# Batch 0 of an attention and mixer kernel written out in program order, with its loads in another order

## The chip, the cores and the metric

The kernel runs on one core of a Trainium2 chip. The metric is device time in microseconds (us), one launch. A core has a matmul engine (PE, with its weight loads shown as PEld), three engines for elementwise work (DVE, ACT, POOL) and SP, which only issues DMAs here. Each engine works through its own instructions in order and waits for others by semaphores. SP and POOL issue DMAs into two different queues; both queues are served by the same 16 DMA engines. Only POOL's DMAs change the type (here from float32 to bfloat16).

## What is computed

Eight batches of causal attention with a decay bias (8 heads, 576 positions, 64 dims), and a mixer on the result:

```python
scores = scale * q @ k.T
cum = cumsum(maximum(s, 0), axis=-1)
bias = minimum(-(cum[:, :, :, None] - cum[:, :, None, :]), 0)
attn = softmax(where(causal, -1e9, scores + bias))
x = (attn @ v)                    # heads side by side: (8, 576, 512)
u = x + (x.T @ U @ V).T           # U (576, 32), V (32, 576): along the sequence
out = u + maximum(u @ w_ch1, 0) @ w_ch2     # w_ch1 (512, 2048), w_ch2 (2048, 512)
```

## The kernel before

**Stages.** Work goes by pairs of heads, four pairs to a batch, 32 in all.

- `scores(n)` (L245): for each head of pair n, matmuls of q and k from a slot into PSUM, with exp on ACT (L264, L273, L277, L279) and the causal mask as a minimum with `keep` on DVE (L265, L285). Results lie in one of two tiles `pT`. The decay bias is in the matmul: rows 64 to 67 of a slot hold the cumulated decay of q and k in split precision, so the contraction is over 68 rows. Nine matmuls, 1600 columns a head.
- `values(n)` (L296): 15 matmuls of 65 columns a head with v, where a column of ones gives the sum; DVE divides (L315, L316) into `x_sb`.
- `seqmix(b)` (L325), once a batch: U (L329), a copy `ux` on DVE (L337), then for each of four blocks a transposition and V (L342, L350) and a DVE cast into `uT` (L358; L378 for the last 64 positions).
- `chanmix(g)` (L386), for 512 tokens: 16 blocks of w1 (four matmuls of 512 columns each, L391) with ReLU on ACT (L398), then four times 16 matmuls with w2 (L404), the residual (L415), a copy on DVE and the store. It is a generator, and its steps are used as filling: `run` (L437) takes one step of filling after each step of scores, values or seqmix; `fill_with(n)` takes n steps at once.

**q and k.** Batch 0's q and k are loaded with positions on 72 partitions (`load_first`, L76) and transposed on PE (`first_transposes`, L202), with copies into the slots on ACT for heads 0 to 3 and on DVE for heads 4 to 7. From batch 1 on, `load_qk` (L85) loads four heads (a group) as 8 DMAs; `place` (L224) transposes 32x32 blocks on DVE (four instructions a group, L234) into `turned` and moves them into a slot by 8 DMAs on SP (L240), with the decay rows from HBM (L226). There are three slots of four heads, four buffers for groups and two for `turned`.

**The beginning.** s is loaded (SP, L67); DVE clamps, scans and splits it (L140 to L147), ACT makes the negated row (L143); SP moves the rows of batch 0's eight heads into slots 0 and 1 (L150), one DMA a head, and the others to HBM (L155). On POOL's queue stand: q and k of heads 0 and 1, 2 and 3, 4 to 7; v of batch 0 (`load_v`, L167: five DMAs of 128-byte rows, after a memset of the tile); U and V; w1 whole (2 MB, L190); q and k of batch 1; w2 whole (2 MB, L192); v of batch 1. POOL's DMAs take turns on eight semaphores, and one is issued only when that which had its semaphore before has landed. `spin` (L129) issues matmuls on constants whose result nobody reads.

**What sets the order.** Each engine's order is set by the framework's scheduler, which takes the source order as a start and moves instructions by its own estimates. So in the built program the first scores stand ahead of the last transposes of heads 4 to 7, the memsets of `v_slot` (L163, L164) stand between the steps of the decay rows on DVE, and group 2's transposes (L234) stand behind `ux`.

Of the kernel before, what the change touches and what calls it, by code (L numbers as in the profile page):

```python
# [20 lines left out]
def kernel(  # L21
# [40 lines left out]

# [4 lines left out]
    nc.sync.dma_start(out=s_sb, in_=s.rearrange("b h s -> (b h) s"))  # L67

# [5 lines left out]
    )  # L74

# [9 lines left out]
    def load_qk(b):  # L85
        for g in range(2 * b, 2 * b + 2):
            qk_t[g] = loads.tile([128, 2, ST * D], BF16, tag="qk_sd", name="qk_sd", bufs=4)
# [6 lines left out]

    load_first(0, 2)
    identity = consts.tile([128, 128], BF16)
    make_identity(nc, identity)
    load_first(2, 2)
    load_first(4, 4)

    keep = consts.tile([128, 4, 128], BF16)
    nc.gpsimd.memset(keep, 3.0e38)
    nc.gpsimd.affine_select(
        out=keep,
        in_=keep,
        compare_op=ALU.is_ge,
        fill=0.0,
        base=0,
        pattern=[[0, 4], [1, 128]],
        channel_multiplier=-1,  # L110
    )


    PW = 1664
    pTs = [consts.tile([128, 2, PW], BF16, name=f"pT{i}") for i in range(2)]
    nc.vector.memset(pTs[1][:, 0, 0:640], 1.0)
    nc.vector.memset(rows[:, 0:3, 0, :], 1.0)
    nc.vector.memset(rows[:, 3, 1, :], 1.0)
    for pT in pTs:
        nc.vector.memset(pT[:, :, 1600:], 1.0)  # L120
    NSLOT = 3

    SK = 5 * 128
    slots = [consts.tile([128, 4, S + SK], BF16, name=f"slot{i}") for i in range(NSLOT)]
    for slot in slots:
        nc.vector.memset(slot[:KA, :, 2 * S :], 0.0)


    def spin(n):  # L129
        for _ in range(n):  # L130
            nc.tensor.matmul(
                pscore(),
                lhsT=pTs[1][:, 0, 512:640],
                rhs=pTs[1][:, 0, 0:512],
                start=True,
                stop=True,
            )


    nc.vector.tensor_scalar(s_sb, s_sb, 0.0, 1.0 / scale, op0=ALU.max, op1=ALU.mult)  # L140
    nc.vector.tensor_tensor_scan(cum, s_sb, s_sb, 0.0, op0=ALU.add, op1=ALU.max)
    rest = s_sb
    nc.scalar.mul(rows[:, 3, 0, :], cum, -1.0)  # L143
    nc.vector.tensor_copy(rows[:, 0, 1, :], cum)
    nc.vector.tensor_sub(rest, cum, rows[:, 0, 1, :])
    nc.vector.tensor_copy(rows[:, 1, 1, :], rest)
    nc.vector.tensor_sub(rows[:, 2, 1, :], rest, rows[:, 1, 1, :])  # L147
    for n in range(PB):
        for hh in range(2):
            nc.sync.dma_start(  # L150
                out=slots[n // 2][D:KA, 2 * (n % 2) + hh, 0 : 2 * S],
                in_=rows[2 * n + hh : 2 * n + hh + 1].rearrange("n r c s -> n r (c s)"),
            )
    rows_hbm = nc.dram_tensor("rows_hbm", (4, BH, 2, S), BF16, kind="Internal").ap()
    nc.sync.dma_start(  # L155
        out=rows_hbm[:, ds(2 * PB, BH - 2 * PB)].rearrange("r n c s -> n r c s"),
        in_=rows[2 * PB :],
    )

    v_slots = []  # L160
    for i in range(3):
        vt = consts.tile([128, 5, H, D + 1], BF16, name=f"v_slot{i}")
        nc.vector.memset(vt[:, :, :, D : D + 1], 1.0)  # L163
        nc.vector.memset(vt[64:, 4, :, :], 0.0)  # L164
        v_slots.append(vt)

    def load_v(b):  # L167
        vt = v_slots[b % 3]
        for t in range(4):
# [5 lines left out]
            out=vt[:64, 4, :, 0:D], in_=v[b, :, 512:576, :].rearrange("h p d -> p h d")  # L175
        )

    load_v(0)
    U_sb = consts.tile([128, 5, 128], BF16)
    nc.vector.memset(U_sb, 0.0)  # L180
    V_sb = consts.tile([128, S], BF16)
# [269 lines left out]
    for n in range(PB):  # L451
        for _ in first_transposes(n):
            spin(1)
# [56 lines left out]
```

## Time and profile before

| | us |
|---|---|
| median of 4 runs | 409.2 (408.21 to 412.18) |
| profiled execution | 409.13 |
| its span, first to last instruction | 407.4 |
| PE busy | 374.2 (92%) |
| DVE, ACT, POOL busy | 195.8, 194.7, 106.6 |
| first scores of batch 0 start on PE | 19.27 |
| first matmul of seqmix(0) | 40.84 |
| first matmul of chanmix(0) | 45.98 |
| first scores of batch 1 start on PE | 56.63 |

The span is counted from the first instruction; the profiled execution's time has 1.7 us around it. A matmul's end is modelled, so PE's busy time is rather too long for short matmuls. In lists of waits a line reads: who waited, for whom, us in total, how often, the longest. In a timeline a line reads: start, us, engine, line, operation, tile written and read, shape, count, and in brackets the idle time before it with what ended it. The granted clock of PE is a share of its full clock.

### The profile page before, as it was taken

What the parts mean: (1) busy time and instruction counts of PE and PEld (TensorE: products, weight loads), DVE (VectorE), ACT (ScalarE), POOL (GpSimd) and SP (SyncE); (2) the same over time, 40 slices, a digit from 0 to 9 for tenths busy, and PEclk for the clock granted to TensorE, in tenths of its full rate; (3) what the DMA queues carried; (4) which work ended last, traced back from release to release, by engine and by line L of the source; (5) the groups of instructions that cost most, each with busy time, mean ns of one, the idle gap of its engine ahead of it and who ended that gap; (6) DMA issues with size and microseconds to landing.
All of it is one profiled execution on the core that took longest, in us unless ns stands there. A gap on an engine that the chain in (4) does not pass through costs nothing.

```text
span 407.4 us, 7986 instructions
## 1 busy us (share of the span) xinstructions
PE 374.2 (92%) x3121; PEld 212.7 (52%) x3176; DVE 195.8 (48%) x394; ACT 194.7 (48%) x378; POOL 106.6 (26%) x171
## 2 busy tenths in 40 slices
PE   6188849999989999999999999999999999999996
PEld 2067425565545555556555655555555554444442
DVE  8168821789588654754574734432444331002011
ACT  4096237653855087327732683358336630630610
POOL 8527328785763764300040000000000000000000
PEclk9557978999999999999999999999999999999999
DMA  8999999999997997572156311220011002001002
GB/s 109 153 224 113 181 159 168 117 209 197 182 157 128 178 174 101 80 101 76 34 62 104 89 35 29 71 69 2 0 53 53 2 0 79 26 26 64 16 27 77
DMA packets 80524, 37.91 MB, mean 93 GB/s; under 512 B 64422, under 2 KB 74822, under 8 KB 80486
## 3 DMA queue, kind: packets, MB, share of 16 engines
q0 software_dynamic: 65680, 18.44, 50.8%
q1 hardware_dynamic: 14806, 18.96, 16.7%
q8 instruction: 25, 0.41, 0.4%
q14 instruction: 13, 0.11, 0.1%
HBM read 37.51 MB, written 9.95 MB: 116 GB/s over the span
## 4 chain that ended last, share of the span: by engine, by line
PE 62%; DMA 21%; DVE 7%; POOL 5%; issue 2%; ACT 1%; SPq 1%; DVEq 0%; POOLq 0%; ACTq 0%
PE pwork L404 25%; PE pwork L391 21%; DMA v_slot<-in_v_dram 9%; PE pscore L253 6%; DVE turned L234 5%; DMA w_sb<-in_moe_w_ch_dram 4%; PE pwork L306 4%; DMA slot<-turned 4%; POOL qk_sd L90 2%; DMA qk_sd<-in_k_dram 2%; DMA hT<-in_k_dram 2%; PE pwork L329 2%; PE pwork L415 2%; PE pwork L342 1%; POOL v_slot L170 1%
## 5 line engine op out<-in xcount | busy, mean ns | idle before, releaser
L391 PE MATMUL pwork<-uT,w_sb 128*128 128x512 bf16 x548 | 141.2, 383 | 3.3 <-DVE x_sb L316 1.9
L404 PE MATMUL pwork<-w_sb,hT 128*128 128x512 bf16 x553 | 138.5, 379 | 1.2
L398 ACT ACTIVATE hT<-pwork 128x512 bf16<-128x512 f32 x144 | 88.0, 612 | 79.7 <-PE pwork L391 76.8
L253 PE MATMUL pscore<-slot 68*128 68x128 bf16 (+4 forms) x576 | 70.9, 254 | 15.3 <-DMA slot<-hT 9.9
L264 ACT ACTIVATE pT<-pscore 128x512 bf16<-128x512 f32 x64 | 38.6, 603 | 96.5 <-PE pscore L253 96.4
L404 PEld LDWEIGHTS <-hT 128*128 128x128 bf16 x576 | 52.3, 98 | 48.1
L391 PEld LDWEIGHTS <-w_sb 128*128 128x128 bf16 x576 | 51.3, 98 | 48.1 <-DVE x_sb L316 2.4
L253 PEld LDWEIGHTS <-slot 68*128 68x128 bf16 x576 | 45.5, 103 | 45.6 <-issue 17.9
L424 DVE COPY o_sb<-pwork 128x512 f32<-128x512 f32 x36 | 24.7, 687 | 79.8 <-PE pwork L415 79.8
L234 DVE STREAM_TRANSPOSE turned<-qk_sd 128x576 bf16<-128x576 bf16 x56 | 59.5, 1121 | 4.9 <-DMA slot<-turned 2.7
L265 DVE TENSOR_TENSOR pT<-pT,keep 128x512 bf16<-128x512 bf16 x64 | 26.7, 421 | 65.4 <-ACT pT L264 65.2
L306 PEld LDWEIGHTS <-pT 128*128 128x128 bf16 x960 | 40.0, 100 | 14.5 <-issue 0.7
L273 ACT ACTIVATE pT<-pscore 128x512 bf16<-128x512 f32 x64 | 39.0, 610 | 13.0 <-PE pscore L253 11.0
L306 PE MATMUL pwork<-v_slot,pT 128*128 128x65 bf16 x960 | 43.1, 197 | 0.3
L170 POOL DMA_DIRECT2D v_slot<-in_v_dram x32 | 28.3, 897 | 55.5 <-PE pwork L306 52.9
L90 POOL DMA_DIRECT2D qk_sd<-in_k_dram x56 | 31.5, 568 | 31.4 <-DMA v_slot<-in_v_dram 18.4
L277 ACT ACTIVATE pT<-pscore 128x512 bf16<-128x512 f32 x64 | 39.3, 614 | 0.1
L90 POOL DMA_DIRECT2D qk_sd<-in_q_dram x56 | 31.7, 581 | 17.2 <-DMA w_sb<-in_moe_w_ch_dram 9.7
L316 DVE TENSOR_TENSOR x_sb<-pwork,rec 128x320 bf16<-128x320 f32 x64 | 30.9, 488 | 1.9
L358 DVE CAST uT<-pwork 128x512 bf16<-128x512 f32 x32 | 21.3, 684 | 9.8 <-PE pwork L350 9.2
L315 DVE RECIPROCAL rec<-pwork 128x5 f32<-128x5 f32 x64 | 11.5, 183 | 29.2 <-PE pwork L306 28.9
L415 PEld LDWEIGHTS <-uT 128*128 128x128 bf16 x144 | 11.1, 98 | 8.5
(54 smaller groups left out, 155.1 us busy)
## 6 DMA issues: line engine op xcount, KB each, us to landing
out_dram<-o_sb SPq DMA_DIRECT2D x36, 256.0 KB
slot<-turned SPq DMA_DIRECT2D x112, 72.0 KB
v_slot<-in_v_dram POOLq DMA_DIRECT2D x32, 128.0 KB, 6.9
w_sb<-in_moe_w_ch_dram POOLq DMA_DIRECT2D x2, 2048.0 KB, 16.4
qk_sd<-in_q_dram POOLq DMA_DIRECT2D x56, 72.0 KB, 4.6
qk_sd<-in_k_dram POOLq DMA_DIRECT2D x56, 72.0 KB, 4.3
v_slot<-in_v_dram POOLq DMA_DIRECT2D x8, 64.0 KB, 7.5
rows_hbm<-hT SPq DMA_DIRECT2D x1, 504.0 KB
```

The costliest lines, as they stand in the source:

```text
L90: nc.gpsimd.dma_start(out=qk_t[g][ds(32 * a, 32), c, :].rearrange("p (n f) -> p n f", n=6), in_=src[b, 4 * (g % 2) + a].rearrange("(n p t) ...
L170: nc.gpsimd.dma_start(out=vt[:, t, :, 0:D], in_=v[b, :, ds(t * 128, 128), :].rearrange("h p d -> p h d"),)
L234: nc.vector.transpose(turned[:, c, e].rearrange("p (n m t) -> p n t m", n=6, t=3), src[:, c].rearrange("p (n t e d) -> p e n t d", n=6, t= ...
L253: nc.tensor.matmul(dst, lhsT=kT[:, ds(j * 128, 128)], rhs=qT[:, lo:hi], start=True, stop=True,)
L264: nc.scalar.activation(pT[:, hh, 0:512], diag, EXP, scale=scale)
L273: nc.scalar.activation(pT[:, hh, 512:1024], far, EXP, scale=scale)
L277: nc.scalar.activation(pT[:, hh, 1024:1536], mid, EXP, scale=scale)
L306: nc.tensor.matmul(po[:, i, :], lhsT=pT[:, hh, ds(spot(j, i), 128)], rhs=vt[:, j, h, :], start=(j == 0), stop=(j == i), skip_group_check=True,
L316: nc.vector.tensor_tensor(x_sb[:, :, ds(h * D, D)], po[:, :, 0:D], rec.to_broadcast([128, 5, D]), op=ALU.mult,)
L391: nc.tensor.matmul(f1, lhsT=w1_sb[:, kt, ds(nf * 128, 128)], rhs=uT[:, kt, ds(g * 512, 512)], start=(kt == 0), stop=(kt == 3),)
L398: nc.scalar.activation(hT[:, nf, :], f1, RELU)
L404: nc.tensor.matmul(f2, lhsT=hT[:, nf, ds(i * 128, 128)], rhs=w2_sb[:, nf, :], start=(nf == 0), stop=False, skip_group_check=True,)
```

## The change

- Everything from the first load to the end of batch 0's seqmix stands in a block in which the scheduler keeps the program's order on every engine. What follows is scheduled as before, and may be moved in between.
- Memsets of ones write pairs as one FP32 value. The spins read a tile of their own, `warm`, and write one PSUM tile, `idle`, which is held to the end of batch 0, so that three of the four `pwork` buffers are left for it. There are 48 spins (10, then 2 + 2 + 8, then one after each step that is run `warmly`) where there were 16.
- The q k loads stand ahead of the identity on POOL. Transposes and copies of heads 0 to 3 stand ahead of the first scores, those of heads 4 to 7 after the scores of pairs 0 and 1. One copy in two of heads 2 and 3 is on DVE.
- The decay rows' DMAs stand ahead of the memsets of `v_slot`, and so ahead of the loads of v.
- w1 and w2 are four tiles of 512 KB each, loaded by four DMAs each (w1 in 1 KB rows, where it had 4 KB). The order of loads is: v of batch 0, U, V, two blocks of w1, q and k of batch 1, two blocks of w1, v of batch 1, w2.
- `turned` holds q and k of one half of the dims side by side, so that a row of its DMA is 2304 bytes, not 1152. Groups have three buffers, not four.
- Eight steps of chanmix(0), not four, are run before batch 1.

In the built program, DVE's order in batch 0 after pair 0's masks is: copies of heads 4 and 5, masks of pair 1, copies of heads 6 and 7, rec and x_sb of pair 0, two masks of pair 2, two transposes of group 2 (they wait for q), the last mask of pair 2, rec and x_sb of pair 1, masks of pair 3 with the other two transposes of group 2 (they wait for k) between them, rec and x_sb of pairs 2 and 3 with two transposes of group 3 between, ux, a transpose of group 3, the uT casts, the last transpose of group 3.

```diff
+    warm = consts.tile([128, 512], BF16)
...
+    w1_sb = [consts.tile([128, 4, 512], BF16, name=f"w1_sb{i}") for i in range(4)]
+    w2_sb = [consts.tile([128, 4, DM], BF16, name=f"w2_sb{i}") for i in range(4)]
...
+    ones_pair = float.fromhex("0x1.007f00p+0")
+
+    def ones(ap):
+        nc.vector.memset(ap.bitcast(FP32), ones_pair)
...
-            qk_t[g] = loads.tile([128, 2, ST * D], BF16, tag="qk_sd", name="qk_sd", bufs=4)
+            qk_t[g] = loads.tile([128, 2, ST * D], BF16, tag="qk_sd", name="qk_sd", bufs=3)
...
+    def load_w1(i):
+        nc.gpsimd.dma_start(
+            out=w1_sb[i],
+            in_=moe_w_ch1[:, ds(i * 512, 512)].rearrange("(kt kp) n -> kp kt n", kp=128),
+        )
...
-        for c in range(2):
-            for e in range(2):
+        for e in range(2):
+            for c in range(2):
                 nc.vector.transpose(
-                    turned[:, c, e].rearrange("p (n m t) -> p n t m", n=6, t=3),
+                    turned[:, e, c].rearrange("p (n m t) -> p n t m", n=6, t=3),
                     src[:, c].rearrange("p (n t e d) -> p e n t d", n=6, t=3, e=2)[:, e],
                 )
-        for a in range(4):
-            for e in range(2):
+            for a in range(4):
                 nc.sync.dma_start(
-                    out=slot[ds(32 * e, 32), a, 0 : 2 * S].rearrange("p (c s) -> p c s", c=2),
-                    in_=turned[ds(32 * a, 32), :, e, :],
+                    out=slot[ds(32 * e, 32), a, 0 : 2 * S],
+                    in_=turned[ds(32 * a, 32), e].rearrange("p c s -> p (c s)"),
                 )
...
-                    lhsT=w1_sb[:, kt, ds(nf * 128, 128)],
+                    lhsT=w1_sb[nf // 4][:, kt, ds(nf % 4 * 128, 128)],
...
-                    rhs=w2_sb[:, nf, :],
+                    rhs=w2_sb[nf // 4][:, nf % 4, :],
...
-    spin(8)
-    for n in range(PB):
-        for _ in first_transposes(n):
-            spin(1)
-    for n in range(PB):
-        drain(scores(n))
-        if n > 0:
-            drain(values(n - 1))
+    copy_a, copy_v = nc.scalar.copy, nc.vector.tensor_copy
+    with tc.manual_schedule():
+        nc.sync.dma_start(out=s_sb, in_=s.rearrange("b h s -> (b h) s"))
+        load_first(0, 2)
+        make_identity(nc, identity)
+        load_first(2, 2)
+        load_first(4, 4)
...
+        ones(warm)
+        ones(rows[:, 0:3, 0, :])
+        ones(rows[:, 3, 1, :])
+        for slot in slots:
+            nc.vector.memset(slot[:KA, :, 2 * S :], 0.0)
+        idle = pwork()
...
+        spin(10)
+        chain = first_transposes(0, (copy_a, copy_a))
+        nc.vector.tensor_scalar(s_sb, s_sb, 0.0, 1.0 / scale, op0=ALU.max, op1=ALU.mult)
+        nc.vector.tensor_tensor_scan(cum, s_sb, s_sb, 0.0, op0=ALU.add, op1=ALU.max)
+        next(chain)
+        spin(2)
+        nc.scalar.mul(rows[:, 3, 0, :], cum, -1.0)
+        drain(chain)
+        spin(2)
...
+        for h in range(H):
+            nc.sync.dma_start(
+                out=slots[h // 4][D:KA, h % 4, 0 : 2 * S],
+                in_=rows[h : h + 1].rearrange("n r c s -> n r (c s)"),
+            )
...
+        for i, vt in enumerate(v_slots):
+            nc.vector.memset(vt[:, :, :, D : D + 1], 1.0)
+            nc.vector.memset(vt[64:, 4, :, :], 0.0)
+            if i == 0:
+                drain(first_transposes(1, (copy_a, copy_v)))
+                spin(8)
...
+        load_v(0)
...
+        load_w1(0)
+        load_w1(1)
+        load_qk(1)
+        load_w1(2)
+        load_w1(3)
+        load_v(1)
+        for i in range(4):
+            load_w2(i)
+
+        def warmly(gen):
+            for _ in gen:
+                spin(1)
+
+        drain(scores(0))
+        warmly(first_transposes(2, (copy_v, copy_v)))
+        drain(scores(1))
+        warmly(first_transposes(3, (copy_v, copy_v)))
+        warmly(values(0))
+        warmly(scores(2))
+        warmly(values(1))
+        warmly(scores(3))
+        warmly(values(2))
+        warmly(values(3))
+        warmly(seqmix(0))
     place(2)
-    drain(values(PB - 1))
-    drain(seqmix(0))
     fill.append(chanmix(0))
-    fill_with(4)
+    fill_with(8)
```

## The prediction

> **What bounds the kernel now.** I read the page's slices first, then the stages with the granted clock, the waits, the chain, and the timelines of PE and DVE.
>
> ```profile
> PE   6188849999989999999999999999999999999996
> PEclk9557978999999999999999999999999999999999
> ```
>
> A slice is 10.2 us. From the sixth slice on PE is full; all that can be won cheaply lies in the first 63 us. The stages (us; PE, PEld, DVE, ACT, POOL busy; then clock, DMA share, GB/s) put bounds on that:
>
> ```profile
> 12.00:35.80 23.80, 15.21 (x165) 12.54 (x166) 11.23 (x27) 13.45 (x26) 10.27 (x18) 0.50 1.45 174
> 46.00:51.50 5.50, 5.43 (x23) 2.23 (x23) 5.36 (x7) 2.88 (x5) 0.00 (x0) 1.00 1.25 204
> 51.50:56.30 4.80, 0.00 (x0) 0.00 (x0) 0.00 (x0) 0.60 (x1) 1.14 (x2) 1.00 2.10 171
> 56.40:63.10 6.70, 6.47 (x28) 3.26 (x29) 3.08 (x5) 4.11 (x9) 2.01 (x4) 0.50 1.76 149
> 63.20:110.90 47.70, 46.74 (x451) 27.93 (x458) 32.90 (x64) 29.27 (x61) 36.69 (x59) 1.00 1.60 175
> ```
>
> After 63.2 PE has 46.7 of 47.7 us at full clock: a microsecond won earlier is one off the end. Before it, two waits of PE and the half clock behind each are the loss:
>
> ```profile
> PE pscore L253 <- DMA slot<-hT: 9.9, 1, 9.9
> PE pscore L253 <- DMA slot<-turned: 5.1, 1, 5.1
> ```
> ```profile
> 19.27 1.01 PE L253 MATMUL pscore<-slot 68*128 68x128 bf16 x6 [9.87 <-DMA slot<-hT]
> 45.98 5.51 PE L391 MATMUL pwork<-uT,w_sb 128*128 128x512 bf16 x23 [0.20 <-DVE uT L358]
> 56.63 1.49 PE L253 MATMUL pscore<-slot 68*128 68x128 bf16 x9 [5.14 <-DMA slot<-turned]
> ```
>
> The first wait is for the decay rows (issued at 11.17, landed at 19.1), the second for batch 1's q and k. Why those are late is in the chain (start, us, what): one 2 MB load of w1 stands before them.
>
> ```profile
> 14.90 16.91 DMA w_sb<-in_moe_w_ch_dram
> 31.81 0.28 issue
> 32.09 4.73 DMA qk_sd<-in_k_dram
> 36.83 0.28 issue
> 37.11 0.57 POOL qk_sd L90
> ```
>
> And DVE shows what must be done between 19.27 and 45.98, and that two transposes of group 2 came late, after ux:
>
> ```profile
> 24.53 6.53 DVE L218 COPY slot<-pwork 64x576 bf16<-64x576 bf16 x8 [3.50 <-PE pwork L210]
> 42.12 0.69 DVE L337 CAST ux<-pwork 128x512 bf16<-128x512 f32 x1 [1.42 <-PE pwork L329]
> 42.73 2.09 DVE L234 STREAM_TRANSPOSE turned<-qk_sd 128x576 bf16<-128x576 bf16 x2
> ```
>
> **Step 1, decay rows ahead of v.** On DVE, ones written as FP32 pairs halve 1728- and 576-wide memsets (1.50+0.54 us to about 1.2), warm (256 words, about 0.3) replaces 0.59, two pT memsets (0.30) move back: the scan's input s, landed at 3.5, is taken at 3.6 and not 4.64. The three memsets of v_slot (0.49 each, 0.17 of gap) leave the chain: it ends at 8.8, not 11.08. ACT's two copies of head 0 (0.80 each) now stand before its negated row (0.68); with the first q k loads issued 0.3 us earlier they end at 8.7, in time. So SP issues the first row at 8.9: 2.3 us won. v_slot's memset follows on DVE, so v is issued from 9.4. Landing: 8.0 us with v in flight (rows of before); 2.7 us for the s load beside the q k loads alone. The first two rows stand ahead of v: I take 3.5 us, near the 2.7, as q k tail and then v packets still run (ends 2.7 and 8.0). Scores of batch 0 start at 12.7 (11.8 to 17), with 10+2+2+8 spins and all transposes of heads 0 to 3 done before; rows 3 to 8 are issued among the v loads and keep 7 us, so pair 1 starts near 17.3. The write of rows_hbm stays behind the eight rows on SP and goes out near 14 (before 19.15); its read-backs are wanted only by batch 1.
>
> The row: 8.0 us behind queued v loads. Against it stands the Trainium skill, "DMA: Bandwidth & Descriptors", Queues, rings and completion order: an engine goes round its queues packet by packet, so a small transfer shouldn't wait for another queue's backlog, and v's place would not matter. By it only the 2.3 us of issue would be won, scores would start at 17, and the sum would be about 405.
>
> **Step 2, batch 0 in program order.** No lead of PE passes on unless DVE passes it on. The built order of DVE's instructions shows what follows pair 0's last mask (about 16.4): copies of heads 4 to 7, 6.5 us; masks of three pairs, 6 x 0.41 + 3 x 0.22 = 3.1; 8 x (0.17+0.48) = 5.2 for rec and x_sb; ux and four uT casts, 0.7 + 2.5; and, new, seven transposes of groups 2 and 3 before the uT casts (before: two), 7 x 1.05 = 7.4. Sum 25.4. Added waits: pair 1's exps, started by the late rows, 1.5 us; and the first transpose, which stands between two masks of pair 2, waits for q of group 2, 2 us (step 3). Behind it on DVE are all masks and rec/x_sb of pairs 1 to 3, and PE's values wait for these. So chanmix(0) starts at 16.4+25.4+3.5 = 45.3, against 45.98: of 6.6 us won in front, 0.7 is left. Ends: 41 (waits and part of the transposes covered) and 50 (q 5 us later).
>
> PE does 48 spins for 16. At full clock a 128x512 takes 0.216 (groups of four follow each other at 0.87 in PE's timeline): 32 x 0.216 = 6.9 us more. 24 of the 48 stand in the DVE-bound stretch from 17 to 45, where PE has about 12 us of work (three pairs' scores 4.2, values 3.6, transposes 1.4, seqmix 3.0) plus 5 of spins in 28: free. At half clock they cost twice and PE comes close to the bound.
>
> **Step 3, load order.** Before w1 lands there are now 1 MB of it ahead of q k. The whole took from about 16 to 31.8; half of it, issued 1.2 us later (16.1), lands near 26. That w2, with 1 KB rows, landed in 15.9 us and w1, with 4 KB rows, in 16.9 says that cutting w1 to 1 KB rows costs the queue nothing that shows (bounds 0 and, if each of two blocks kept a 2 us landing of its own, 2). q of group 2 then lands at 28.5, its last k, issued once w1's second block is down, 4.7 us after 26.3 (row of before: 32.09 to 36.83), at 31; group 3 by 35 (before 40.4). POOL issues eight DMAs of about 0.8 us for w1 and w2 in place of two; it is held by landings (9.3 us at w1, 9.7 at w2), so these six cost nothing unless it were the issue that is late, and then 4.8 us behind q k, where nothing is waiting. w1's other half (needed at block 9 of chanmix, 52) lands near 40, v (needed at 64) near 46, w2 (needed at 64) near 56: all covered by 8 us or more. qk buffers go from 4 to 3; group 5 then waits for group 2's transposes, done by 36, long before its turn at 58.
>
> Group 2's transposes end at 35.5, SP issues its eight rows by 38.8 (0.6 each; 2304-byte rows, half the packets), and with v in flight (7 to 9 us, as at 49.15 to 56.5) they land by 46. Scores of pair 4 come after eight blocks of chanmix, 45.3 + 6.9 = 52: the stall of 5.1 us is gone with 6 us in hand. In later batches the larger rows can only shorten waits like DVE's 2.2 us at 112, behind which PE lost 1.5: 0 to 1.5, and I take nothing. With no gap the clock does not fall either: at half clock 6.6 us of PE work were done from 56.63 to 63.18, which at full clock take 3.3.
>
> **Step 4, what is paid.** fill_with(8) for 4: the built order of PE shows scores, values and the seqmix of batch 1 with no chanmix block among them; in batch 0 such a seqmix took 45.98 - 40.84 = 5.1 us for 3.0 of matmuls (7168 columns at 0.216 per 512); in batch 1 PE now loses 0.5 of the 8 us from 93 to 101. So 0.5 to 3 lost; I take 1.5. And the clock: it takes a nearly full stretch to be granted (0.50 from 12.0 to 35.8, though PE was 64% busy). Ten spins at 0.43 (eight were done in the 3.5 us before the grant at 5.15) are 4.3 us of it, where sixteen were 6.8; if it isn't granted in batch 0, seqmix costs 2 us more and chanmix's first 3.4 to 6.8 us run at half, 1.7 to 3.4 us. Ends 0 and 5.4; I take 1.2, nearer to nothing, as spins stand in every stretch and PE busy for 7.1 of 10.1 us held the clock from 35.9 to 46.0.
>
> The row is the clock granted at 5.15 after spins from 1.66. The Trainium skill, "TensorE: Matmul & The Clock Gate", Part 1, speaks against the ten spins: the window is 3.4 us, free-running, and must be busy throughout, so 4.3 us of spins would hold a whole one in a quarter of the runs only (an estimate). By it alone the clock would cost nearer 4, and the sum would be 405.5.
>
> **Sum,** against the profiled execution (407.4 span, 1.7 around it, 409.1; the median of the runs shown is 409.2): - 0.7 - 5.1 - 3.3 + 1.5 + 1.2 = - 6.4, so 402.7.
>
> **Rivals.**
> - *The whole lead passes on.* q lands by 26 and DVE's waits vanish: chanmix starts at 40.5 to 41. For: 6.6 us are won in front, DVE is only 69% busy from 19.27 to 45.98. Against: five more transposes stand before uT. 402.7 - 4.6 = 398, or 397 with the clock kept.
> - *The clock stays at half,* or the rows still land late: + 4.2 for the clock's upper end, 407. For: ten spins, DVE-bound gaps. Against: 48 spins.
> - *DVE stands behind q k* (slower). The transpose between pair 2's masks is the place: each us that q lands after 28.5 is a us on the end. v goes out 3 us later and w1 as 1 KB rows; if q came at 39 (34 before), chanmix would start at 55.8: 402.7 + 10.5 = 413. Loss begins at 35, and is over 1% from 39. Against: half of w1 no longer stands before it.
>
> **How the numbers follow.** Forecast 0.52 (own range 399 to 405.5), lead passes on 0.18, clock 0.22, slower 0.08. The range runs from 396.5, the bottom of the second, to 408, the top of the third. One per cent is 4.1 us, about what a measurement of this kernel can tell from no change. Faster (under 405.0): 0.48 + 0.18 + 0.03 = 0.69; slower (over 413.3): 0.07; within: 0.24.
>
> **What would show it.** Step 1: first scores at 12 to 13, SP's row issue near 8.9. Step 2: DVE with few gaps from 16 to 45 and a transpose waiting on a q load before pair 2's last mask; chanmix's first matmul at 45. Step 3: no wait for slot<-turned at the first scores of batch 1, clock 1.00 there; w1's first two blocks landed by 26 to 27. Step 4: a gap of 1 to 3 us on PE at batch 1's seqmix. I would be wrong if chanmix begins by 41 or after 49, or if PE waits for w2 or v.

## The result, and the profile after

The changed kernel takes 410.8 us (median of 54 executions, 408.0 to 413.3), the kernel before 409.7 (78 executions beside them). The ratio is 1.0047, 95% interval 1.0034 to 1.0061: slower by half a per cent. Some executions fall in a slower state of the chip; the ratios leave them out, and so do the medians of e10 and e11 below, where they were several. The forecast was 402.7 with a range from 396.5 to 408, and it was wrong.

The page of the changed kernel, PE's busy share and granted clock in 40 slices of 10.2 us:

```profile
PE   6896997975998999999999999999999999999996
PEclk9777999896999999999999999999999999999999
```

Slices two and six, where the page of before has a 1 and a 4 for PE, hold 8 and 9 now. New dents have come behind them: a 7 in slice seven (61 to 72), 7 and 5 in slices nine and ten (82 to 102), with a clock of 0.6 in the tenth. The front did what was forecast. These are the rows of PE's and DVE's timelines (start, us, what, idle time before with its releaser): first scores, the wait for group 2's q, chanmix(0), first scores of batch 1.

```profile
12.95 0.86 PE L190 MATMUL pscore<-slot 68*128 68x128 bf16 x9 [1.05 <-DMA slot<-hT]
...
44.96 7.07 PE L328 MATMUL pwork<-uT,w_sb 128*128 128x512 bf16 x32
51.87 0.42 PE L190 MATMUL pscore<-slot 68*128 68x128 bf16 x5
```
```profile
29.43 2.11 DVE L172 STREAM_TRANSPOSE turned<-qk_sd 128x576 bf16<-128x576 bf16 x2 [1.97 <-DMA qk_sd<-in_q_dram]
```

There is no wait at 51.87, where the kernel before waited 5.14 us at 56.63. The stages side by side show where the lead went (us; PE, PEld, DVE, ACT, POOL busy; then clock, DMA share, GB/s). The kernel before:

```profile
45.00:69.00 24.00, 18.05 (x103) 9.20 (x105) 10.52 (x17) 13.27 (x26) 9.05 (x16) 0.86 1.56 176
69.00:76.00 7.00, 6.95 (x76) 4.13 (x76) 2.56 (x8) 5.28 (x11) 5.90 (x10) 1.00 2.24 129
76.00:86.00 10.00, 9.89 (x106) 6.02 (x105) 9.88 (x18) 3.53 (x7) 8.60 (x14) 1.00 1.22 147
86.00:101.00 15.00, 14.41 (x136) 8.68 (x137) 13.38 (x26) 6.37 (x13) 9.06 (x16) 1.00 1.66 206
```

The changed kernel:

```profile
45.00:69.00 24.00, 23.84 (x172) 12.94 (x175) 5.45 (x10) 18.01 (x37) 9.01 (x16) 1.00 1.43 167
69.00:76.00 7.00, 4.60 (x41) 2.47 (x39) 6.84 (x15) 0.54 (x2) 7.00 (x11) 0.76 1.58 147
76.00:86.00 10.00, 9.89 (x95) 5.96 (x96) 4.64 (x9) 4.48 (x9) 5.48 (x10) 1.00 1.84 202
86.00:101.00 15.00, 8.06 (x85) 5.31 (x85) 13.60 (x28) 5.20 (x12) 12.38 (x20) 0.77 1.68 187
```

From 45 to 69 PE does 5.8 us more, at full clock. From 69 to 101 it does 8.7 us less, 22.55 of 32 where before did 31.25, part of it at half clock. DVE is what PE waits for, and DVE waits for loads. Its timeline has two pairs of transposes with a long wait ahead of them, and PE's has what came of it:

```profile
66.75 2.11 DVE L172 STREAM_TRANSPOSE turned<-qk_sd 128x576 bf16<-128x576 bf16 x2 [7.94 <-DMA qk_sd<-in_q_dram]
68.72 0.40 DVE L202 TENSOR_TENSOR pT<-pT,keep 128x512 bf16<-128x512 bf16 x1
...
85.29 2.11 DVE L172 STREAM_TRANSPOSE turned<-qk_sd 128x576 bf16<-128x576 bf16 x2 [5.27 <-DMA slot<-turned]
```
```profile
71.84 0.61 PE L243 MATMUL pwork<-v_slot,pT 128*128 128x65 bf16 x15 [2.40 <-DVE x_sb L253]
...
96.98 0.58 PE L266 MATMUL pwork<-x_sb,U_sb 128*128 128x512 bf16 x1 [4.55 <-DVE x_sb L253]
```

The first is group 4, the first half of batch 2's q and k. Batch 2 is not wanted before pair 8, but in the built program these transposes stand between the two masks of pair 5, and the second mask (its exp was done at 60.8), all of pair 6's and the values of pair 4 are queued behind them. In the kernel before the built order has them behind pair 6's masks, at 75.45, when q (landed at 63.7) was long there:

```profile
75.06 0.22 DVE L285 TENSOR_TENSOR pT<-pT,keep 128x128 bf16<-128x128 bf16 x1
75.45 2.13 DVE L234 STREAM_TRANSPOSE turned<-qk_sd 128x576 bf16<-128x576 bf16 x2 [0.18 <-DMA v_slot<-in_v_dram]
```

The source calls `place(4)` at the same place in both, ahead of pair 6's scores. The scheduler, which goes by its own estimates, put these transposes behind that place in the kernel before and ahead of it in the changed kernel; between the two lie a pair and a half of masks. The second wait is group 6, the first half of batch 3. It needs its q, and the buffer of `turned` that group 4's rows must have left. The profile names rows leaving `turned`, but group 4's had all landed at 82.4, and the last of four loads of q landed at 85.01: it is a wait for a load as well (e8 tells it apart).

The chain of work that ended last (start, us, what) says the same: from 38 to 97 there is no PE in it.

```profile
37.73 15.92 DMA v_slot<-in_v_dram
...
54.49 11.98 DMA qk_sd<-in_q_dram
...
66.75 1.37 DVE turned L172 x2
...
73.43 7.09 DMA slot<-turned
80.54 4.76 DMA slot<-turned
85.29 2.11 DVE turned L172 x2
...
96.98 0.58 PE pwork L266
```

And the kernel before had it in its own chain, further on than the lines that the prediction quotes:

```profile
41.42 20.28 DMA v_slot<-in_v_dram
...
70.44 7.22 DMA v_slot<-in_v_dram
...
81.85 4.21 DMA qk_sd<-in_k_dram
...
87.02 7.80 DMA v_slot<-in_v_dram
```

So it was loads and their issue on POOL, not PE, that ended last there from 41 to 95, though PE was busy for 46.7 of the 47.7 us from 63.2 to 110.9.

### The profile page after: what moved, and what is told of

It reads as the page before. It is cut to its first block, busy times and chain, and to the rows that moved or that the text cites. A ratio compares the mean times of both kernels' runs of the same rounds, so it can differ in the third digit from the quotient of the medians.

```text
span 409.1 us, 8049 instructions
## 1 busy us (share of the span) xinstructions
PE 380.4 (93%) x3150; PEld 213.9 (52%) x3208; DVE 196.1 (48%) x396; ACT 192.5 (47%) x376; POOL 110.9 (27%) x177
## 4 chain that ended last, share of the span: by engine, by line
PE 67%; DMA 15%; DVE 8%; POOL 3%; issue 3%; ACT 2%; SPq 1%; DVEq 0%; ACTq 0%; POOLq 0%
PE pwork L328 24%; PE pwork L341 24%; PE pscore L190 7%; DVE turned L172 6%; PE pwork L243 4%; DMA v_slot<-in_v_dram 4%; DMA slot<-turned 3%; DMA qk_sd<-in_q_dram 3%; DMA w_sb<-in_moe_w_ch_dram 3%; PE pwork L266 2%; PE pwork L279 2%; PE pwork L352 2%; POOL qk_sd L107 1%; PE pwork L287 1%; DMA hT<-in_k_dram 1%
## 5 line engine op out<-in xcount | busy, mean ns | idle before, releaser
L341 PE MATMUL pwork<-w_sb,hT 128*128 128x512 bf16 x555 | 141.1, 382 | 1.1
L328 PE MATMUL pwork<-uT,w_sb 128*128 128x512 bf16 x550 | 138.7, 379 | 1.7 <-DVE x_sb L253 0.3
L328 PEld LDWEIGHTS <-w_sb 128*128 128x128 bf16 x576 | 51.2, 98 | 46.6 <-DVE x_sb L253 0.8
L190 PE MATMUL pscore<-slot 68*128 68x128 bf16 (+4 forms) x576 | 67.1, 244 | 2.1 <-DMA slot<-hT 1.1
L190 PEld LDWEIGHTS <-slot 68*128 68x128 bf16 x576 | 44.0, 99 | 33.4 <-issue 2.7
L243 PEld LDWEIGHTS <-pT 128*128 128x128 bf16 x960 | 38.8, 100 | 21.2 <-issue 6.0
L243 PE MATMUL pwork<-v_slot,pT 128*128 128x65 bf16 x960 | 41.6, 197 | 7.0 <-DVE x_sb L253 3.6
L115 POOL DMA_DIRECT2D v_slot<-in_v_dram x32 | 28.3, 899 | 38.1 <-PE pwork L243 36.5
L107 POOL DMA_DIRECT2D qk_sd<-in_k_dram x56 | 31.8, 575 | 23.9 <-DMA w_sb<-in_moe_w_ch_dram 13.1
L253 DVE TENSOR_TENSOR x_sb<-pwork,rec 128x320 bf16<-128x320 f32 x64 | 31.2, 488 | 2.1
L266 PE MATMUL pwork<-x_sb,U_sb 128*128 128x512 bf16 x38 | 11.8, 437 | 8.7 <-DVE x_sb L253 8.4
## 6 DMA issues: line engine op xcount, KB each, us to landing
w_sb<-in_moe_w_ch_dram POOLq DMA_DIRECT2D x8, 512.0 KB, 13.7
```

What stands on the lines that cost most here:

```text
L107: nc.gpsimd.dma_start(out=qk_t[g][ds(32 * a, 32), c, :].rearrange("p (n f) -> p n f", n=6), in_=src[b, 4 * (g % 2) + a].rearrange("(n p t) ...
L115: nc.gpsimd.dma_start(out=vt[:, t, :, 0:D], in_=v[b, :, ds(t * 128, 128), :].rearrange("h p d -> p h d"),)
L190: nc.tensor.matmul(dst, lhsT=kT[:, ds(j * 128, 128)], rhs=qT[:, lo:hi], start=True, stop=True,)
L243: nc.tensor.matmul(po[:, i, :], lhsT=pT[:, hh, ds(spot(j, i), 128)], rhs=vt[:, j, h, :], start=(j == 0), stop=(j == i), skip_group_check=True,
L253: nc.vector.tensor_tensor(x_sb[:, :, ds(h * D, D)], po[:, :, 0:D], rec.to_broadcast([128, 5, D]), op=ALU.mult,)
L328: nc.tensor.matmul(f1, lhsT=w1_sb[nf // 4][:, kt, ds(nf % 4 * 128, 128)], rhs=uT[:, kt, ds(g * 512, 512)], start=(kt == 0), stop=(kt == 3),)
```

## The experiments

All times are medians, each with its ratio to the kernel before on the same chip in the same minutes (that kernel took 407.9 to 410.5) and a 95% interval. The theory, called H: DVE takes its instructions in order, transposes that the scheduler put ahead of their data hold up masks and values, and that gives the lead back. Against it: F, `fill_with(8)` uses up the blocks that batch 1's seqmix needs; D or L, the load stream paces everything to 130 us, wherever the transposes stand.

### e1: group 4's transposes put back

```diff
+    with tc.manual_schedule(engines={DVE}):
+        for n in range(PB, 2 * PB):
...
+            if hp % 2 == 0 and n != PB:     # behind values(n - 1)
+                place(n // 2 + 1)
```

> The changed kernel with one thing moved: DVE takes batch 1 in program order and the four transposes of group 4 stand behind pair 6's masks and the values of pair 5, as they did in the kernel before (there the built order has them in that place), and not between the two masks of pair 5. Theory H (DVE's order gives the lead back: the wait of 7.9 us for batch 2's q at 58.8 holds pair 5's second mask, and PE with it, at 69): the wait is gone or under 1 us, PE is busy through 69 to 76 (5.5 of 7 us or more, 4.6 before), and of the 10 us lost from 69 to 101 six come back: 403.5 to 406 against 410.8. Rival F (fill_with(8) leaves batch 1's seqmix without work to fill it): unchanged, 409.5 to 411.5. Rival D (the loads are the bound until 73, so PE waits for group 4's q and k wherever the transposes stand): PE waits 4 us or more for slot<-turned at the first scores of batch 2, 408 to 411.

405.1 us, ratio 0.992 (0.988 to 0.995). H's range holds it. The stage from 69 to 76 is full again, and PE waits for group 4's rows at pair 8, as D had it, but for 3.6 us and not for all:

```profile
69.00:76.00 7.00, 6.95 (x73) 4.30 (x73) 4.51 (x10) 2.84 (x6) 7.00 (x11) 1.00 1.67 157
76.00:86.00 10.00, 6.37 (x62) 3.67 (x61) 8.33 (x16) 2.45 (x5) 7.89 (x14) 0.92 1.38 220
86.00:101.00 15.00, 14.32 (x124) 8.68 (x125) 12.07 (x23) 7.39 (x15) 9.76 (x16) 0.83 1.93 185
```
```profile
84.61 0.64 PE L190 MATMUL pscore<-slot 68*128 68x128 bf16 x5 [3.58 <-DMA slot<-turned]
```

So DVE's order in batch 1, with group 4's place in it, is worth 5.7 us by the medians, 5.3 by the ratios.

### e2: the fill

```diff
-    fill_with(8)
+    fill_with(4)
```

> The changed kernel with fill_with(4) in place of 8. The built order then has group 4's transposes behind pair 5's second mask, ahead of the values of pair 4. Theory H: DVE still stands until q lands at 66.5, with values of pair 4 behind it where pair 5's mask was; 408.5 to 411.5. Rival F: batch 1's seqmix has chanmix blocks beside it again, the 4.5 us wait at 97 and the half clock around it go: 404 to 407. Rival D: unchanged, 409.5 to 411.5.

409.2 us, ratio 1.002 (1.000 to 1.005), as H had it. DVE waits 6.7 us for the same q, and PE stands for 6.2 us, until 68.2, in one piece:

```profile
65.50 2.08 DVE L172 STREAM_TRANSPOSE turned<-qk_sd 128x576 bf16<-128x576 bf16 x2 [6.74 <-DMA qk_sd<-in_q_dram]
```
```profile
68.19 1.89 PE L328 MATMUL pwork<-uT,w_sb 128*128 128x512 bf16 x4 [6.21 <-DVE x_sb L253]
```

### e3: the old order of loads

```diff
-        load_w1(0); load_w1(1); load_qk(1); load_w1(2); load_w1(3); load_v(1); w2
+        w1 (four blocks); load_qk(1); w2 (four blocks); load_v(1)
```

> The changed kernel with the loads in the order of the kernel before: w1 whole (in four blocks), q and k, w2, v. Everything else is as changed. Theory H: group 2's q lands near 36, chanmix(0) starts 5 us or more later, but that lead was given back at 69 in any case, since batch 2's q lands near 66 in both: 410 to 414. If the lead were kept to the end, as the prediction had it, the loss would be 6 us or more: 417 or more.

411.5 us, ratio 1.009 (1.006 to 1.012). H's range holds it. Taking back the whole load order costs 0.7 us by the medians, 1.7 by the ratios: most of the lead that it had bought was not kept in any case.

### e4: the kernel before with the new loads alone

```diff
-    nc.gpsimd.dma_start(out=w1_sb, ...)
-    load_qk(1)
-    nc.gpsimd.dma_start(out=w2_sb, ...)
-    load_v(1)
+    load_w1(0); load_w1(1); load_qk(1); load_w1(2); load_w1(3); load_v(1)
+    for i in range(4):
+        load_w2(i)
```

> The kernel before with the weights in blocks and the new load order alone (its batch 0 as the scheduler puts it, rows behind v). The built order has group 4's transposes between pair 5's two masks, as in the changed kernel. Theory H: the stall of 5.1 us for slot<-turned at batch 1's first scores is gone, and the wait of DVE for batch 2's q appears and takes it back: 407 to 412. Prediction's view of the loads (stall and half clock gone, 8.4 us less the clock): 401 to 404.

403.5 us, ratio 0.990 (0.987 to 0.994). H missed this, since it had misread the built order. Group 4 stands between pair 6's masks there, DVE comes to it later (67.7), q has landed at 63.1, and there is no wait:

```profile
67.69 2.11 DVE L251 STREAM_TRANSPOSE turned<-qk_sd 128x576 bf16<-128x576 bf16 x2
```

The time lies in the range of the prediction's view, 401 to 404: where DVE doesn't stand in the way, the load order gains, 4.0 us by the ratio and some 5 by the medians, of the 8.4 that step 3 gave it. With the rest of the change on top of it the time is 7.3 us longer.

### e5: U's memset early

```diff
             if i == 0:
+                nc.vector.memset(U_sb, 0.0)
+                nc.vector.memset(V_sb, 0.0)
                 drain(first_transposes(1, (copy_a, copy_v)))
```

> The changed kernel with the two memsets of U and V moved up on DVE, from behind the copies of heads 2 and 3 to right behind v_slot 0's. In the changed kernel POOL waits 2.2 us for U's memset before its load (issued at 15.3, in the kernel before and in e4 at 12.5), and everything behind it on POOL's queue, w1 to batch 2's q, comes that much later. If the load stream is shifted as a whole: w1's first block issued near 14.5, batch 2's q landed at 63 to 64.5 (66.5), DVE's wait shorter by 2 to 3 us, 407.5 to 409.5 against 410.8. If the queue catches up before batch 2's q, since it is full throughout: q at 66 again, 410 to 411.5.

409.8 us, ratio 1.001 (0.998 to 1.004). w1 was issued at 15.0 (17.1), yet its first block landed at 24.4 (24.2) and batch 2's q at 66.8 (66.5): the queue catches up. POOL's wait of 2.4 us for U's memset costs nothing.

### e6, e7: group 4 earlier, U early

```diff
 (e1, U's memset early)
-                place(n // 2 + 1)           # behind values(n - 1)
+                place(n // 2 + 1)           # between scores(n) and values(n - 1)
 e6: DVE in program order through pair 8; e7: through pair 7
```

> e1 and e5 together, with group 4's transposes one step earlier than in e1: behind pair 6's masks and ahead of the values of pair 5 (DVE in program order through pair 8, so group 5's stand behind pair 8's masks). In e1 group 4's transposes ran from 74.0, though k had landed at 68.1, and PE waited 3.6 us for the rows and had 6.8 us of half clock behind that. Theory H: no wait of PE over 1 us before 101 but at batch 1's seqmix, clock 1.00 from 57 on, and the 7 us that e1 still lost come back but for the DVE work put ahead of values: 398 to 402. Rival D (the loads bound this stretch): 404 or more.

> As e6, but only group 4's transposes are held in place and the scheduler takes DVE back after pair 7, so that group 5's follow at once, among pair 5's values and pair 7's masks. Group 5's q lands 3.5 to 5 us after group 4's (70.3 and k 73.4 in e1, some 2.5 us sooner here). Theory H: these transposes come near the landing and DVE waits 1 to 3 us again with pair 7's masks behind it: 400 to 404, 1 to 3 us over e6. Rival D: as e6 within 1 us.

410.1 us, ratio 1.003 (0.999 to 1.006), and 409.9, ratio 1.000 (0.997 to 1.004). H missed both, by 8 and 6 us; D's ranges (404 or more, and e7 as e6) hold both, so here the load stream was still open as the bound. Group 4 went well in both (PE 7 of 7 us from 69 to 76); then group 5 did in e6 what group 4 had done:

```profile
86.64 4.01 DVE L172 STREAM_TRANSPOSE turned<-qk_sd 128x576 bf16<-128x576 bf16 x4 [0.28 <-DMA qk_sd<-in_q_dram]
```
```profile
92.19 0.58 PE L266 MATMUL pwork<-x_sb,U_sb 128*128 128x512 bf16 x1 [4.18 <-DVE x_sb L253]
```

Four transposes ahead of pair 7's values, for which batch 1's seqmix waits. In e7 it was group 6, whose place the scheduler chose again: a wait of 4.9 us for batch 3's q at 86.3, then PE idle for 5.7 us at 95.5.

### e8: a third buffer of turned

```diff
-        turned = work.tile([128, 2, 2, S], BF16, tag="turned", name="turned")
+        turned = work.tile([128, 2, 2, S], BF16, tag="turned", name="turned", bufs=3)
```

> The changed kernel with three buffers of turned in place of two: group 6's transposes no longer wait (5.3 us at 80.0 to 85.3) for the rows of group 4 to leave. The first wait of 7.9 us at 58.8 stays. If the second wait is a loss of its own, PE's 4.5 us at 97 and the half clock around it shrink: 406 to 408.5. If it only passes on the first wait (DVE, released earlier, stands at the next load or row), 409.5 to 411.5.

409.6 us, ratio 1.000 (0.997 to 1.003). The wait stays, 4.7 us to 85.3, though no row of `turned` is in its way any more: batch 3's q landed at 85.0 here too. The expectation had taken over the profile's name for it.

### e9, e10: DVE's order as in e4, through pair 8

```diff
+    AT = {6: 4, 7: 5, 8: 6}      # at pair n: group; one half after the first head's scores,
+    ...                          # one after the first head's values
+    with tc.manual_schedule(engines={DVE}):
+        for n in range(PB, 2 * PB + 1):
 e9: fill_with(4); e10: fill_with(8); both with U's memset early
```

> The changed kernel's batch 0 (rows ahead of v, program order, U's memset early as in e5) with batch 1's DVE order as it was built in e4: group 4's transposes in two halves, behind pair 6's first mask and between the two heads of pair 5's values, groups 5 and 6 likewise one and two pairs on, and fill_with(4). At 69 the changed front stands 3.4 us further than e4 in matmul columns left (301.5 against 304.9 us at 2.4 columns a ns). If DVE's order alone gave the lead back: 403.5 - 3.4 = 400, 399 to 401.5. If the loads are the bound until 101 whatever stands in front, the lead runs dry at batch 2's first scores or at batch 1's seqmix: 402.5 to 406.

> e9 with fill_with(8). The same work, four chanmix blocks sooner. If the fill matters (rival F: batch 1's seqmix without blocks beside it): 3 to 6 us over e9, with a wait of PE at batch 1's seqmix and half clock behind it. If DVE's order is all: within 1.5 us of e9.

408.7 us, ratio 0.998 (0.994 to 1.001), and 411.3, ratio 1.002 (0.998 to 1.006). e9 is outside both of its ranges, and e10 lies 2.6 us over it by the medians, 1.6 by the ratios, between what the fill and what DVE's order would give. e9 starts batch 1's seqmix at 89.7, as e4 (89.1), and loses 6 us on e4 after it, where the scheduler orders DVE again. The profile names the rows for this wait too, but it is group 8's, and batch 4's q landed at 104.3:

```profile
104.41 1.13 DVE L172 STREAM_TRANSPOSE turned<-qk_sd 128x576 bf16<-128x576 bf16 x1 [4.10 <-DMA slot<-turned]
```
```profile
106.91 1.55 PE L329 MATMUL pwork<-uT,w_sb 128*128 128x512 bf16 x4 [3.52 <-DVE x_sb L254]
```

### e11: less to load

```diff
+        if n == PB + 1:
+            place(4)                         # ahead of pair 5's masks
-        for i in range(4):
-            load_w2(i)
+        load_w2(0)
...
-                    rhs=w2_sb[nf // 4][:, nf % 4, :],
+                    rhs=w2_sb[0][:, nf % 4, :],
```

Three of w2's four blocks are left out, and the first is used for all.

> The changed kernel with group 4's transposes held ahead of pair 5's masks (all four, a little sooner than in the changed kernel) and only the first of w2's four blocks loaded and used for all (the second layer is computed with wrong weights: 1.5 MB, about 8 us of queue, is left out). Batch 2's q then lands near 58 in place of 66.5. If DVE's wait for the landing is the loss at 69: the wait is under 2 us, PE full from 57 to 76, and 403 to 406. If it is the 4.2 us of transposes themselves standing ahead of pair 5's masks and values: 408 to 411 as in the changed kernel.

409.5 us, ratio 0.997 (0.992 to 1.003); these executions spread from 404.9 to 410.4. q landed at 59.1, DVE waited 2.1 us until 59.4, and PE was full from 57 to 76, as the landing theory said. The time missed its range and lies in that of the rival, by which the transposes themselves, 4.2 us ahead of pair 5's masks, cost; but they stood there with PE full. The next long wait is group 6's for batch 3's q:

```profile
78.52 2.09 DVE L172 STREAM_TRANSPOSE turned<-qk_sd 128x576 bf16<-128x576 bf16 x2 [6.99 <-DMA qk_sd<-in_q_dram]
```

After these misses two explanations were left, hoisting (the scheduler moving up) of whichever group comes next, or a load stream that paces everything.

### e12 to e15: a square with DVE's order held

DVE takes the whole main loop in program order, each group in two halves at a fixed pair. From group 4 on, DVE's order is the same in all four; batch 0 and the load order are new or old.

```diff
+    AT = {PB: 3, PB + 2: 4}
+    AT.update({2 * g - 3: g for g in range(5, NP // 2)})
+    with tc.manual_schedule(engines={DVE}):
+        for n in range(PB, NP + 1):
+            step(n)                          # halves of place(AT[n]) after the first step
...                                          # of scores(n) and of values(n - 1); fill_with(4)
 e13, e15: loads as in e3
 e14, e15: batch 0 as before (e4's file, fill_with(4); place and three group buffers as changed)
```

> DVE in program order through the whole main loop, with every group's transposes held in two halves at one place (group 4 at pair 6, group 5 at pair 7, each later group g at pair 2g-3), so that the scheduler hoists none of them; fill_with(4); batch 0 and the loads as changed. Part of a square of four with the same DVE order from batch 1 on: front new or old, loads new or old. Theory H (transposes hoisted ahead of their loads or of a free buffer are what gives the lead back, at group 4, and at group 8 in e9): no wait of DVE over 2 us between 57 and 130, 399 to 402.5. Rival L (the load stream paces everything until 130): as the square's old front with new loads within 1.5 us, 402.5 to 406.

> As e12 with the loads in the old order (w1 whole, q k, w2, v, in the same blocks). Theory H: by matmul columns left at 69 the old order stood 2.8 us behind the new (304.3 in e3, 301.5 in e1): 402 to 405.5. Rival L: within 1.5 us of the old front with old loads.

> As e12 with batch 0 as in the kernel before (scheduled, rows behind v), new load order. Theory H: at 69 the old front with new loads stood 3.4 us behind the new front (304.9 in e4, 301.5 in e1): 402.5 to 406, 3 to 4 us over e12. Rival L: e12 within 1.5 us.

> As e12 with batch 0 and the load order of the kernel before: the kernel before with its DVE order held, the new place and w1 and w2 in blocks. Theory H: 309.3 left at 69 before, 4.4 us behind e4: 406 to 410, 4 us over e14 and 7 us over e12. Rival L: within 2 us of e13.

| us (ratio, 95% interval) | loads new | loads old |
|---|---|---|
| batch 0 new | e12 395.0 (0.969, 0.965 to 0.974) | e13 400.8 (0.982, 0.979 to 0.985) |
| batch 0 old | e14 398.3 (0.976, 0.972 to 0.980) | e15 403.1 (0.987, 0.985 to 0.990) |

L falls: it had e12 and e14 within 1.5 us of each other, and e13 and e15 within 2. The load order is worth 4.8 to 5.8 us and batch 0's program order 2.3 to 3.3, and all four are faster than the kernel before, e12 by more than 2%. H had the signs, and the size for e14 over e12 (3.4 expected, 3.3 measured) and e15 over e14 (4.4 and 4.8); it had too little for e13 over e12 (2.8 and 5.8). Its level was too slow: all four lie 1 to 4 us below the low ends of its ranges. Part of that is waits after 101 that the held order ends too: PE is busy for 35.00 of the 35 us to 136 in all four, 33.59 in the changed kernel and 34.16 in e4. The stages of e12, with the same loads as the changed kernel:

```profile
45.00:69.00 24.00, 24.00 (x207) 13.41 (x205) 10.42 (x23) 18.10 (x37) 10.84 (x19) 1.00 1.54 175
69.00:76.00 7.00, 7.00 (x74) 4.28 (x72) 6.91 (x13) 3.53 (x7) 6.67 (x10) 1.00 1.89 161
76.00:86.00 10.00, 10.00 (x99) 5.83 (x96) 6.24 (x14) 3.53 (x7) 5.64 (x10) 1.00 1.53 227
86.00:101.00 15.00, 15.00 (x148) 8.93 (x147) 10.44 (x20) 10.91 (x23) 11.79 (x17) 1.00 1.68 177
101.00:136.00 35.00, 35.00 (x331) 20.33 (x327) 22.32 (x43) 16.73 (x34) 15.01 (x25) 1.00 1.15 126
```

PE is never idle from 45 to 136, and its chain from 46 to 110 consists of PE alone. From 45 to 101 the loads went at nearly the same rate in both, 183 GB/s here and 176 in the changed kernel (worked out from the four rows of each): what differed is when they were waited for.

### e16 to e18: what in the held order does it

```diff
 e16 (e12)
-    fill_with(4)
+    fill_with(8)
 e17 (the changed kernel): one line around the main loop, nothing moved in the source
+    with tc.manual_schedule(engines={mybir.EngineType.DVE}):
 e18 (e17): place(n // 2 + 1) behind values(n - 1)
```

> e12 with fill_with(8) as in the changed kernel: the change unaltered but for the place of the transposes on DVE. Rival F (eight blocks used up leave batch 1's seqmix bare): 2 us or more over e12, 397 to 400, with a wait of PE at batch 1's seqmix. By DVE's order alone: within 1 us of e12's 395.

> The changed kernel with one line put around its main loop, which makes DVE take it in program order; the transposes stay where the source calls for them, all four of a group in one piece ahead of an even pair's masks (group 4 ahead of pair 6's, group 5 ahead of pair 8's and so of the values of pair 7 that batch 1's seqmix waits for), fill_with(8). If it is only the hoisting that costs: 395 to 397. If the piece of 4.2 us ahead of a pair's masks and values costs by itself, as group 5's did in e6 (PE waited 4.2 us at batch 1's seqmix, then 6.8 us of half clock): 400 to 406.

> As e17 with each group's four transposes behind the values of that step in place of ahead of its scores (group 4 behind pair 5's values, group 5 behind pair 7's, ahead of batch 1's seqmix casts). No masks or values of the step stand behind them, but rows leave later: as in e1, PE waits near 4 us for group 4's rows at pair 8's scores, with half clock behind it. 398 to 403; if that wait is covered, 395 to 397.

e16: 396.8 us, ratio 0.972 (0.969 to 0.975). e17: 396.7, ratio 0.972 (0.969 to 0.975). e18: 414.0, ratio 1.015 (1.011 to 1.020).

e17 is the cleanest of all. PE's weight loads and ACT's instructions come in the changed kernel's order, one for one, in the two traces; DVE's order differs, and with it that of SP's and POOL's DMAs. Its stages from 45 to 101:

```profile
45.00:69.00 24.00, 24.00 (x179) 12.90 (x175) 10.42 (x19) 17.84 (x36) 11.79 (x20) 1.00 1.49 182
69.00:76.00 7.00, 7.00 (x72) 4.18 (x71) 3.99 (x12) 3.17 (x7) 5.75 (x10) 1.00 2.05 166
76.00:86.00 10.00, 9.83 (x126) 6.62 (x124) 8.14 (x17) 5.68 (x12) 6.94 (x12) 1.00 1.36 209
86.00:101.00 15.00, 14.42 (x124) 8.03 (x123) 10.36 (x21) 8.95 (x19) 10.31 (x16) 1.00 1.61 143
```

Batch 0 has no part in it: chanmix(0) starts at 45.14 in e17, 44.96 in the changed kernel. One line takes 14.2 us off the changed kernel (13.4 by the ratios). Halves or whole pieces make no difference here (e16 and e17 agree), and the fill is worth 1.1 us by the ratios of e12 and e16, 1.8 by their medians, less than the 2 at which F was to begin. e18, which missed its range by 11 us, shows that program order is no merit by itself. Behind the values of a batch's last pair the transposes stand ahead of ux, for which PE waits six times in the whole run, and rows leave too late four times:

```profile
PE pwork L287 <- DVE ux L274: 8.9, 6, 2.4
PE pscore L190 <- DMA slot<-turned: 5.1, 4, 2.6
```

e12 and e17 beat both kernels; e12, the fastest, by 13.7 us on the kernel before.

Where each kernel stood, from the traces (start of batch 1's seqmix on PE, first copy of chanmix(1)'s output on DVE, end of PE's work):

| us | seqmix(1) | first output of chanmix(1) | end |
|---|---|---|---|
| before | 94.0 | 125.0 | 403.3 |
| changed | 97.0 | 125.7 | 404.9 |
| e1 | 93.8 | 123.2 | 400.3 |
| e4 | 89.1 | 118.2 | 397.1 |
| e6 | 92.2 | 124.6 | 404.4 |
| e9 | 89.7 | 124.8 | 404.1 |
| e12 | 84.9 | 113.6 | 389.1 |
| e13 | 91.7 | 120.4 | 395.9 |
| e14 | 87.4 | 116.0 | 391.5 |
| e15 | 92.8 | 121.5 | 397.0 |
| e17 | 86.8 | 115.9 | 389.9 |
| e18 | 91.6 | 122.7 | 407.8 |

## Why the prediction was wrong, by its own steps

**The step that failed** is in the part on what bounds the kernel: "After 63.2 PE has 46.7 of 47.7 us at full clock: a microsecond won earlier is one off the end." A busy share says that PE had work, not that the work would have been there sooner. PE got to pair 5 earlier, DVE got with it to transposes whose q had not come, and stood for 7.9 us. The runs show in its place that a lead lasts where DVE's order is held: in e12 to e15 leads of 2.5, 6.8 and 7.9 us at batch 1's seqmix (e12 against e14, e13, e15) are 2.4, 6.8 and 7.9 at the end. So it left out one condition, and that was on hand twice: the chain of waits of the kernel before consists of loads from 41 to 95, and the built orders show where group 4's transposes stand. The prediction read the built order of batch 0 and of batch 1's seqmix, and not what lies between. None of the signs that it named for being wrong came (chanmix by 41 or after 49, PE waiting for w2 or v): they look at the front, and the loss lies behind it.

**Step 1, right.** Rows were issued at 8.87 (forecast 8.9) and scores began at 12.95 (12.7). The first row took 4.0 us, near the 3.5 taken and between the ends 2.7 and 8.0. One of v's five loads, issued at 8.67, stood ahead of it, against the step's 9.4; in the kernel before all five did, and it took 8. By the rule of the Trainium skill ("DMA: Bandwidth & Descriptors", Queues, rings and completion order), as the step read it, scores would have begun at 17; the measurement decides against that. That it was v's place which made the difference is the likely reading, but no run moves v alone.

**Step 2, right in its numbers.** chanmix(0) began at 44.96 (45.3), a transpose waited for q of group 2 for 1.97 us (2) between pair 2's masks.

**Step 3, half right.** Scores of pair 4 began at 51.87 (52) without a wait, at full clock, so the 5.1 and 3.3 us were won. Group 2's q landed at 29.3 and its k at 31.2 (28.5 and 31). Further back the landings slipped: w1's first half at 28.3 (26), its other half at 46.6 (40), v at 54.1 (46), w2 at 64.5 (56). Each was hidden, as forecast, but batch 2's q, which stood behind them, landed at 66.5, which the step did not price: it has group 5's turn for a buffer at 58 and nothing on who waits for the load. In the kernel before that q had landed at 63.7. The third rival names the mechanism, DVE behind q and k, for group 2 alone.

**Step 4, right for the fill.** It was to cost 1.5 us and costs 1.1 to 1.8 (e12 against e16). The clock was half for 17 us in batch 0, 23.9 before, and not at all from 41.8 to 72.5. What the clock in batch 0 was worth, priced at 1.2, no run tells apart. The losses after 69 come on top.

**The sum.** With the transposes out of the way the change gains what was forecast: from e15 (batch 0 and load order as before, DVE held, fill 4) to e16 (the change with its fill of 8, DVE held) the time falls by 6.3 us, the forecast was 6.4. That they agree so well is partly luck: the sum had 8.4 for the load order, which the square puts at 4.8 to 5.8, and 0.7 less 1.2 for batch 0, which it puts at a gain of 2.3 to 3.3. The 8.1 us between forecast and result, and some 6 more, are the scheduler's order: 14 us by the medians of the changed kernel and e16, 13.4 by their ratios.

**What is shown, and what is open.** The Trainium skill, "PSUM — Partial Sum Buffer", Engine vs sequencer instructions, says that the queues of ScalarE, VectorE and GpSimdE are strictly first in, first out; the trace agrees: pair 5's second mask, whose exp was done at 60.8, ran at 68.7, behind the transposes that waited until 66.75. That the load stream paces everything (L) is refuted by e12, the buffers of `turned` by e8, U's memset by e5. Whether group 4's early place alone costs all 5.7 us of e1, or the later groups' places that moved with it a part, was not tried apart.

## What to carry to other kernels

An engine that runs ahead meets loads sooner: before pricing a lead, follow the chain of waits over the whole stretch in which the lead is to last, and for every prefetching step on an in-order engine set the time at which the engine now gets there against the time at which its data lands. Look in the built order for instructions that a scheduler moved ahead of what the next wait depends on; one line that holds an engine to its program order was worth more in the changed kernel (14 us) than the whole rewrite of the front and its loads (8 us, e15 to e12); with the old front and loads it was worth some 5 (e15 against the kernel before, with weights in blocks and the new `place`). A poor place in that order cost as much (17 us from e17 to e18). When a wait that is taken away only comes back elsewhere, as in e6 to e11, hold the whole order and not one place in it.

## What the runs showed of the hardware

The clock was granted and taken in steps of 3.41 us: half clock from 72.49 to 75.90 and from 92.97 to 99.79 in the changed kernel, 84.38 to 91.21 in e1. The Trainium skill, "TensorE: Matmul & The Clock Gate", Part 1, gives such a free-running window of 3413 ns, and says that the full clock comes after at least one busy window. One was not always enough here. Worked out from PE's records, as the columns started in each window over those that the granted clock can stream, e12 had it back after one window of 1.02 (23.56 to 26.97), but e17 only after four of 1.02, 0.94, 1.05 and 0.99 (11.57 to 25.23), and the kernel before after two of 0.95 and 0.98 (56.35 to 63.18). In the changed kernel the stall of 2.4 us that ended at 71.84 cost one window, that of 4.6 us that ended at 96.98 two; what sets the number, no run here tells.
